# Rearranging the first chunk of a fused linear-attention and MLP kernel: PSUM banks, load order, attention slots and constants

## The chip, the cores and the metric

The kernel runs on one core of a Trainium2 chip. The metric is the device time in microseconds of one execution. The kernel before takes 301.79 us (median of 3 runs, 301.38 to 301.83). A profile is one execution taken by the hardware profiler; its span is some 1.8 us shorter than the time (299.9 us for the kernel before, in an execution of 301.66 us). Times within a profile count from the start of its span.

## The reference, cut to what matters

```
phi(x) = where(x > 0, x, exp(x) - 1) + 1          # q, k, v: 8 batches, 8 heads, 576 tokens, 64 wide
kv  = sum over tokens of phi(k) v                  z = sum over tokens of phi(k)
num = phi(q) kv                                    den = phi(q) z + 1e-6
x = num / den, heads side by side                  # 4608 tokens x 512
h = x @ w_in ; g = h - tanh(h) ; out = g @ w_out   # 512 -> 2048 -> 512
```

Inputs and output are float32; the kernel multiplies in bfloat16. A load from GpSimd's queue casts on its way (18.35 MB counted on that queue for 36.7 MB of inputs).

## The kernel before

TensorE is busy nearly all the time, so the kernel runs the two layers of the MLP without a break, in 9 chunks of 512 tokens, and slips the attention of later batches between their matmuls. A chunk has a first layer (16 blocks of 4 matmuls, each block followed by a tanh on ScalarE and a subtraction on VectorE) and a second layer (16 steps of 4 matmuls). Lists `s1[block]` and `s2[step]` hold what is emitted after a block or a step. In the traces each engine runs its instructions in the order in which the kernel emits them (in the changed kernel VectorE subtracts for the tenth block at 27.48 us and does what stands in that block's slot at 28.09 us), so a slot in these lists is also a place in VectorE's and ScalarE's queues.

The divisor of the attention has to be spread from one row per head to 64 rows per head. Batches 0 and 1, which are urgent, do that by matmuls with a selector ("spread"); later batches send 1/den out to memory and read it back broadcast (`ds`, then `rdb`).

The opening, with the PSUM banks it uses (first index of the free part of `ps_all`):

```
def b0_z(i):        # sum of phi(k):  ps_all[:, 2*i + hg, 0:32]
def b0_kv(i):       # phi(k) v:       ps_all[:, 4 + 2*i + hg, 0:128]
def b0_num(i, ns):  # numerators:     banks 2 and 3; the last 64 tokens in bank 1
    ...
def b0_spread(pairs, n0):          # 1/den of two head pairs into banks 4 to 7
    for n, p in enumerate(pairs):
        for t in range(4):
            nc.tensor.matmul(ps_all[:, 4 + t, 128 * (n0 + n):128 * (n0 + n) + 128], sel..., rden...)
def b0_scale(p, ns, n):            # x of one head pair = numerator * spread
    nc.vector.tensor_mul(xT[:, p, 0:512]..., ns[:, p, 0:8]..., ps_all[:, 4:8, 128 * n:128 * n + 128]...)
...
b0_spread((0, 2), 0); b0_scale(0, ns0, 0); b0_scale(2, ns0, 1)
b0_num(1, ns0)
b0_spread((1, 3), 2); b0_scale(1, ns0, 2); b0_scale(3, ns0, 3)
```

The loads, in the order of GpSimd's queue:

```
load_q(0); make_identity(nc, ident); load_k(0); load_v(0)
for g in range(4): load_wi(g)
load_k(1); load_wo(0); load_wo(1); load_q(1); load_wo(2); load_v(1); load_wo(3)
```

The slots of chunk 0, in which batch 1 is worked off, and of chunk 1 (`n1` is batch 2 there):

```
s2[3].append(lambda: a_qphi(1, 0)); s2[5].append(lambda: a_qphi(1, 1))
s2[6].append(lambda: a_qT_pe(1, 0, side)); s2[7].append(lambda: a_qT_pe(1, 1, side))
s2[10].append(lambda: a_kv(1, side))
s2[12].append(lambda: (a_den(1, side), num1(), a_split(1)))
s2[14].append(lambda: spread1(0))
s2[15].append(lambda: (spread1(1), a_qphi(2, 0), a_qphi(2, 1), a_qT_dma(2)))
...
s1[8 if c == 1 else 5].append(lambda: a_kv(n1, attn))
s1[11 if c == 1 else 8].append(lambda: (a_den(n1, attn), a_spread(n1)))
for p in range(NP + 1):
    s2[(11 if c == 1 else 9) + p].append(lambda p=p: a_num(n1, p))
```

## Time and profile before

| | before |
|---|---|
| time | 301.79 us |
| span of the profile | 299.9 us |
| TensorE busy | 288.8 us, 96% |
| VectorE, ScalarE, GpSimd busy | 181.9, 150.2, 48.7 us |
| first matmul of the first layer | 19.24 us |
| chunk 0, second layer begins | 33.07 us |
| chunk 1, first layer begins | 52.57 us |
| chunk 1, second layer begins | 70.05 us |
| chunk 2 begins | 86.25 us |

TensorE is the bound. What can be won is the time in which it stands still, and that lies in the first 86 us alone. So the way to read this profile is not by shares of the span, but stage by stage: where a stage is longer than its matmuls, and what ended the wait there. The prediction below shows those lines.

### The profile page before, as it was taken

To read this page: it belongs to the slowest core of one execution; us is meant where nothing else is said; L and a number is where in the kernel's file an instruction comes from. 1 tells how busy PE (TensorE), PEld (TensorE's weight loads), DVE (VectorE), ACT (ScalarE), POOL (GpSimd) and SP (SyncE) were. 2 spreads that over 40 slices of the span, in tenths; PEclk is the share of its full clock that TensorE was granted. 3 is DMA by queue.
4 is the path that set the end of the run, shared out by engine and by line. 5 is a ranking of instruction groups with operands and counts; after the bars stand their busy time and mean duration, and the time that the engine had idled before them with its cause. 6 is when DMAs were issued, how large, how long until landed. Compare 5 with 4: busy or idle time off the path is not lost.

```text
span 299.9 us, 4765 instructions
## 1 busy us (share of the span) xinstructions
PE 288.8 (96%) x1804; PEld 137.4 (46%) x1804; DVE 181.9 (61%) x320; ACT 150.2 (50%) x234; POOL 48.7 (16%) x87
## 2 busy tenths in 40 slices
PE   8889999989989999999999999999999999999994
PEld 3444453444435444544454445444544444444443
DVE  4769936997467854785478557865682467007600
ACT  4637836856434653565256625662562166126411
POOL 8823150060015000600060006000000000000000
PEclk9999999999999999999999999999999999999999
DMA  6999999669889776968696777977108310131033
GB/s 96 183 206 213 205 206 221 161 99 163 193 185 158 135 177 142 153 114 191 142 148 118 193 150 102 173 182 160 37 4 192 73 35 0 37 77 28 0 72 70
DMA packets 39126, 38.95 MB, mean 130 GB/s; under 512 B 16896, under 2 KB 33856, under 8 KB 38336
## 3 DMA queue, kind: packets, MB, share of 16 engines
q0 software_dynamic: 17600, 18.35, 38.2%
q1 hardware_dynamic: 21504, 20.31, 29.8%
q8 instruction: 14, 0.23, 0.3%
q14 instruction: 8, 0.07, 0.1%
HBM read 43.91 MB, written 9.55 MB: 178 GB/s over the span
## 4 chain that ended last, share of the span: by engine, by line
PE 83%; DMA 6%; DVE 6%; POOL 2%; issue 1%; ACT 1%; SPq 0%; DVEq 0%; POOLq 0%; ACTq 0%
PE ps_all L356 38%; PE ps_all L371 35%; PE ps_all L179 3%; DMA rdb<-ds 3%; DMA kraw<-in_k_dram 2%; PE ps_all L307 2%; DMA ds<-rden 2%; PE ps_all L566 1%; DVE gT L362 1%; PE ps_all L263 1%; POOL qraw L88 1%; DVE kp L138 1%; DVE xT L349 1%; DVE rden L275 1%; POOL kraw L88 1%
## 5 line engine op out<-in xcount | busy, mean ns | idle before, releaser
L356 PE MATMUL ps_all<-xT,w_in_sb 128*128 128x512 bf16 x576 | 127.9, 379 | 0.0
L371 PE MATMUL ps_all<-w_out_sb,gT 128*128 128x512 bf16 x560 | 127.7, 379 | 0.0
L362 DVE TENSOR_TENSOR gT<-ps_all,th 128x512 bf16<-128x512 f32 x144 | 96.4, 686 | 47.8 <-ACT th L361 47.2
L361 ACT ACTIVATE th<-ps_all 128x512 f32<-128x512 f32 x144 | 85.2, 597 | 52.0 <-PE ps_all L356 45.2
L356 PEld LDWEIGHTS <-w_in_sb 128*128 128x128 bf16 x576 | 55.1, 98 | 66.4 <-issue 0.9
L371 PEld LDWEIGHTS <-gT 128*128 128x128 bf16 x560 | 54.2, 98 | 65.6 <-issue 1.7
L377 ACT COPY osb<-ps_all 128x512 f32<-128x512 f32 (+1 forms) x37 | 21.2, 577 | 83.6 <-PE ps_all L371 66.7
L318 DVE TENSOR_TENSOR xT<-ps_all,rdb 128x512 bf16<-128x512 f32 x24 | 16.3, 688 | 15.8 <-PE ps_all L307 12.2
L107 POOL DMA_DIRECT2D v<-in_v_dram x32 | 19.3, 647 | 7.6 <-DMA w_out_sb<-in_moe_w_out_dram 2.3
L136 ACT ACTIVATE e<-qraw 128x1152 bf16<-128x1152 bf16 x16 | 18.4, 1160 | 2.2 <-DMA qraw<-in_q_dram 2.2
L367 POOL COPY g<-gT 1x1 bf16<-1x1 bf16 x5 | 0.9, 176 | 109.4 <-DVE gT L362 109.4
L138 DVE TENSOR_TENSOR kp<-e,r 128x1152 bf16<-128x1152 bf16 x15 | 11.4, 757 | 12.0 <-ACT e L136 11.1
L136 ACT ACTIVATE e<-kraw 128x1152 bf16<-128x1152 bf16 x15 | 17.4, 1161 | 0.0
L138 DVE TENSOR_TENSOR qp<-e,r 128x1152 bf16<-128x1152 bf16 x16 | 12.1, 758 | 7.8 <-ACT e L136 6.9
L179 PE MATMUL ps_all<-v,kp 64*128 64x192 bf16 x252 | 11.8, 243 | 1.2 <-DVE kp L138 1.2
L179 PEld LDWEIGHTS <-kp 64*128 64x128 bf16 x252 | 10.0, 94 | 4.5 <-issue 2.5
L307 PE MATMUL ps_all<-qT,kz 128*128 128x512 bf16 x28 | 10.1, 379 | 1.2 <-DVE xT L318 1.2
L420 PE MATMUL ps_all<-zero 128*128 128x512 bf16 x32 | 9.3, 452 | 1.2 <-DVE zero L384 1.2
L92 POOL DMA_DIRECT2D qraw<-in_q_dram x14 | 8.7, 634 | 8.8 <-DVE r L137 4.9
L92 POOL DMA_DIRECT2D kraw<-in_k_dram x14 | 8.7, 626 | 8.2 <-ACT th L361 4.9
L188 DVE TENSOR_TENSOR kz<-ps_all,mask 128x320 bf16<-128x320 f32 x14 | 6.2, 484 | 5.2 <-PE ps_all L179 5.2
L137 DVE TENSOR_SCALAR r<-qraw 128x1152 bf16<-128x1152 bf16 x16 | 7.3, 454 | 2.2 <-DMA qraw<-in_q_dram 2.2
(78 smaller groups left out, 98.6 us busy)
## 6 DMA issues: line engine op xcount, KB each, us to landing
out_dram<-osb SPq DMA_DIRECT2D x70, 128.0 KB
rdb<-ds SPq DMA_DIRECT2D x12, 576.0 KB
v<-in_v_dram POOLq DMA_DIRECT2D x32, 144.0 KB, 8.0
kraw<-in_k_dram POOLq DMA_DIRECT2D x14, 288.0 KB, 5.0
qraw<-in_q_dram POOLq DMA_DIRECT2D x14, 288.0 KB, 7.2
w_in_sb<-in_moe_w_in_dram POOLq DMA_DIRECT2D x4, 512.0 KB, 10.9
w_out_sb<-in_moe_w_out_dram POOLq DMA_DIRECT2D x4, 512.0 KB, 16.6
qraw<-in_q_dram POOLq DMA_DIRECT2D x4, 144.0 KB, 3.9
```

Of the source, the lines that this page charges most:

```text
L92: nc.gpsimd.dma_start(out=t[64 * hg:64 * hg + 64].rearrange("p i h j d -> p (i h) (j d)"), in_=src[b, 4 * hg:4 * hg + 4].rearrange("h (p j ...
L107: nc.gpsimd.dma_start(out=v_b[b % 2][64 * hg:64 * hg + 64, i, 0:2].rearrange("p h j d -> p h (j d)"), in_=v[b, h0:h0 + 2].rearrange("h (p ...
L136: return (lambda: nc.scalar.activation(e, x, AF.Exp), lambda: nc.vector.tensor_scalar(r, x, 0.0, 1.0, ALU.max, ALU.add), lambda: nc.vector ...
L138: lambda: nc.vector.tensor_tensor(y, e, r, ALU.min))
L179: nc.tensor.matmul(ps[hg], kp[r, i, j].rearrange("p h d -> p (h d)"), vt[r, i, :, j, :], start=(j == 0), stop=(j == J - 1))
L307: nc.tensor.matmul(ps, kz[:, p // 2, p % 2, 0:128], qT[:, p % 2, 0:8, p // 2, :], start=True, stop=True)
L318: nc.vector.tensor_mul(xT[:, p, S * b:S * b + 512].rearrange("p (j t c) -> p j t c", j=8, t=4), ps.rearrange("p j (t c) -> p j t c", t=4), ...
L356: nc.tensor.matmul(h, w_in_sb[:, p, fi * 128:(fi + 1) * 128], xT[:, p, c * 512:(c + 1) * 512], start=(n == 0), stop=(n == NP - 1))
L361: nc.scalar.activation(th, h, AF.Tanh)
L362: nc.vector.tensor_sub(gT[:, fi, :], h, th)
L371: nc.tensor.matmul(o, gT[:, fi, i * 128:(i + 1) * 128], w_out_sb[:, fi, :], start=(fi == 0), stop=(fi == NF - 1))
L377: nc.scalar.copy(osb[:, f0:f1], o[:, f0:f1])
```

## The change

The intent: let the opening wait for less (kv and numerators in banks 0 to 3, the spread in banks 4 to 7, two first-layer matmuls between the two spreads), bring the attention of batch 1 half a layer forward so that its last steps don't stand at the end of chunk 0, load q of batches 1 and 2 ahead of w_out so that this is possible, and take two memsets off VectorE.

```diff
     def b0_z(i):
-                nc.tensor.matmul(ps_all[:, 2 * i + hg, 0:32], ...
+                nc.tensor.matmul(ps_all[:, 4 + 2 * i + hg, 0:32], ...
     def b0_kv(i):
-                nc.tensor.matmul(ps_all[:, 4 + 2 * i + hg, 0:128], ...
+                nc.tensor.matmul(ps_all[:, 2 * i + hg, 0:128], ...
     def b0_num(i, ns):
-        for hg in range(2):
-            nc.tensor.matmul(ps_all[:, 1, 64 * hg:64 * hg + 64], ...      # the last 64 tokens
...
-            nc.tensor.matmul(ps_all[:, 2 + hg, :]...
+            nc.tensor.matmul(ps_all[:, b0 + hg, :]...                     # b0 = 2 * i
-        nc.scalar.copy(ns[:, i::2, 8, :], ...
-    def b0_scale_rest(ns):
+    def b0_scale_rest(banks):
+        ps = num_mm(0, NP, banks)                                         # the last 64 tokens, later
     load_q(0)
+    load_k(0)
     make_identity(nc, ident)
-    load_k(0)
...
     load_k(1)
+    load_q(1)
+    for i in (1, 0):
+        nc.gpsimd.memset(v_b[i][:, :, 2], 1.0)
     load_wo(0)
     load_wo(1)
-    load_q(1)
+    load_v(1)
     load_wo(2)
-    load_v(1)
-    load_wo(3)
...
-            s1[6].append(lambda: b0_scale_rest(ns0))
-            s1[12].append(lambda: a_kphi(1, 0))
...
+            s1[9].append(lambda: b0_scale_rest(first))
+            s1[10].append(lambda: a_kphi(1, 0))
+            s1[12].append(lambda: a_kphi(1, 1))
+            s1[14].append(lambda: a_qphi(1, 0))
+            s2[1].append(lambda: (a_qphi(1, 1), load_q(2), load_wo(3), load_k(2), load_v(2)))
+            s2[2].append(lambda: a_qT_pe(1, 0, side))
+            s2[3].append(lambda: a_qT_pe(1, 1, side))
+            s2[4].append(prepare)
+            s2[5].append(lambda: a_kv(1, side))
+            s2[7].append(lambda: a_den(1, side))
+            s2[8].append(lambda: (num1(), a_split(1)))
+            s2[10].append(lambda: (spread1(0), a_qphi(2, 0)))
+            s2[12].append(lambda: (spread1(1), a_qphi(2, 1), a_qT_dma(2)))
+            s2[15].append(lambda: a_kphi(2, 0))
...
-            s1[8 if c == 1 else 5].append(lambda: a_kv(n1, attn))
-            s1[11 if c == 1 else 8].append(lambda: (a_den(n1, attn), a_spread(n1)))
+            s1[6 if c == 1 else 5].append(lambda: a_kv(n1, attn))
+            s1[9 if c == 1 else 8].append(lambda: (a_den(n1, attn), a_spread(n1)))
...
-            s1[4].append(lambda: a_kphi(2, 0))
-            s1[5].append(lambda: a_kphi(2, 1))
+            s1[1].append(lambda: a_kphi(2, 1))
...
-            first = Banks([4, 5, 6, 7, 0, 1, 2, 3])
+            first = Banks([4, 5, 6, 7, 0, 1, 2, 3, 2, 4, 5, 6, 7])
+                if n == 1:
+                    open2()                    # second spread, after two first-layer matmuls
```

The two memsets and the selector work on VectorE are gone from the opening; the selector work is now `prepare`. Chunk 1 no longer interleaves its first four blocks.

More of the change, by code (lines that the diff above doesn't have):

```diff
@@ L195, in b0_z @@
                 r = slice(64 * hg, 64 * hg + 64)
-                nc.tensor.matmul(ps_all[:, 2 * i + hg, 0:32], kp_t[0][r, i, j].rearrange("p h d -> p (h d)"),
+                nc.tensor.matmul(ps_all[:, 4 + 2 * i + hg, 0:32], kp_t[0][r, i, j].rearrange("p h d -> p (h d)"),
                                  one[r, 0:32], start=(j == 0), stop=(j == J - 1))
     def b0_zc(i):
-        nc.vector.tensor_mul(kz_t[0][:, :, i, 128:160], ps_all[:, 2 * i:2 * i + 2, 0:32], mask[:, :, i, 128:160])
+        nc.vector.tensor_mul(kz_t[0][:, :, i, 128:160], ps_all[:, 4 + 2 * i:6 + 2 * i, 0:32], mask[:, :, i, 128:160])
     def b0_kv(i):
@@ L206, in b0_kv @@
                 r = slice(64 * hg, 64 * hg + 64)
-                nc.tensor.matmul(ps_all[:, 4 + 2 * i + hg, 0:128], kp_t[0][r, i, j].rearrange("p h d -> p (h d)"),
+                nc.tensor.matmul(ps_all[:, 2 * i + hg, 0:128], kp_t[0][r, i, j].rearrange("p h d -> p (h d)"),
                                  v_b[0][r, i, 0:2, j, :], start=(j == 0), stop=(j == J - 1))
     def b0_kz(i):
-        nc.vector.tensor_mul(kz_t[0][:, :, i, 0:128], ps_all[:, 4 + 2 * i:6 + 2 * i, 0:128], mask[:, :, i, 0:128])
+        nc.vector.tensor_mul(kz_t[0][:, :, i, 0:128], ps_all[:, 2 * i:2 * i + 2, 0:128], mask[:, :, i, 0:128])
     def b0_num(i, ns):
-        kz, qT = kz_t[0], qT_t[0]
+        kz, qT, b0 = kz_t[0], qT_t[0], 2 * i
         for hg in range(2):
-            nc.tensor.matmul(ps_all[:, 1, 64 * hg:64 * hg + 64], kz[:, hg, i, 0:128], qT[:, i, 8, hg, :],
-                             start=True, stop=True)
-        for hg in range(2):
-            nc.tensor.matmul(ps_all[:, 2 + hg, :].rearrange("p (j t) -> p j t", j=8), kz[:, hg, i, 0:128],
+            nc.tensor.matmul(ps_all[:, b0 + hg, :].rearrange("p (j t) -> p j t", j=8), kz[:, hg, i, 0:128],
                              qT[:, i, 0:8, hg, :], start=True, stop=True)
-        nc.scalar.copy(ns[:, i::2, 8, :], ps_all[:, 1, 0:128].rearrange("p (a t) -> p a t", a=2))
-        nc.scalar.copy(ns[:, i::2, 0:8, :].rearrange("p a j t -> p a (j t)"), ps_all[:, 2:4, :])
+        nc.scalar.copy(ns[:, i::2, 0:8, :].rearrange("p a j t -> p a (j t)"), ps_all[:, b0:b0 + 2, :])
     def b0_spread(pairs, n0):
@@ L239, in b0_rest @@
     def b0_rest():
-        nc.vector.reciprocal(rden_t[0][:, 128:144], ps_all[:, 0, 128:144])
         ds = dram.tile([H, 4, 16], F32, name="ds0")
@@ L250, in b0_rest @@
         rdb_t[0] = rdb
-    def b0_scale_rest(ns):
+    def b0_scale_rest(banks):
+        ps = num_mm(0, NP, banks)
         nc.vector.tensor_mul(
             xT[:, :, 512:576].rearrange("p a (t c) -> p a t c", t=4),
-            ns[:, :, 8, :].rearrange("p a (t c) -> p a t c", t=4), rdb_t[0])
+            ps[:, 0:NP, :].rearrange("p a (t c) -> p a t c", t=4), rdb_t[0])
     def a_den(b, banks):
@@ L273, in a_den @@
         rden = rpool.tile([128, J * 16], F32, name="rden")
-        n = J * 16 if b > 0 else 128
-        nc.vector.reciprocal(rden[:, 0:n], den[:, 0:n])
+        nc.vector.reciprocal(rden, den)
         rden_t[b] = rden
@@ L419, in spin @@
         for _ in range(n):
-            nc.tensor.matmul(ps_all[:, 2, :], zero[:, 0:128], zero, start=True, stop=True)
-    for t in range(4):
-        nc.scalar.copy(s8[32 * t:32 * t + 32, 0].rearrange("q h p -> q (h p)"),
-                       ident[32 * t:32 * t + 32, 32 * t:32 * t + 8])
+            nc.tensor.matmul(ps_all[:, 0, :], zero[:, 0:128], zero, start=True, stop=True)
     side = Banks([4, 5, 6, 7])
@@ L439 @@
         f()
+    for t in range(4):
+        nc.scalar.copy(s8[32 * t:32 * t + 32, 0].rearrange("q h p -> q (h p)"),
+                       ident[32 * t:32 * t + 32, 32 * t:32 * t + 8])
     nc.scalar.copy(sel, s8[:, 0].rearrange("q h p -> q p h").unsqueeze(3).to_broadcast([128, NP, 2, 64]))
@@ L449 @@
     b0_zc(1)
-    a_den(0, Banks([0]))
+    a_den(0, Banks([4]))
     ns0 = new_ns(0)
+    b0_rest()
     b0_num(0, ns0)
@@ L454 @@
     b0_kz(1)
-    b0_rest()
     b0_spread((0, 2), 0)
@@ L459, with open2, prepare @@
     b0_num(1, ns0)
-    b0_spread((1, 3), 2)
-    b0_scale(1, ns0, 2)
-    b0_scale(3, ns0, 3)
-    nc.vector.memset(v_b[1][:, :, 2], 1.0)
-    nc.vector.memset(v_b[0][:, :, 2], 1.0)
-    for t in range(4):
-        nc.vector.tensor_copy(s8[32 * t:32 * t + 32, 1:3].rearrange("q n h p -> q (n h p)"),
-                              ident[32 * t:32 * t + 32, 32 * t + 8:32 * t + 24])
-    s24 = rpool.tile([128, 2 * NP], F32, name="s24")
-    f8 = s8.rearrange("q n h p -> q n (h p)")
-    nc.vector.tensor_add(s24, f8[:, 1], f8[:, 2])
-    nc.vector.tensor_reduce(part[:, 0:1], s24, mybir.AxisListType.X, ALU.add, negate=True)
-    nc.vector.tensor_reduce(part[:, 1:2], f8[:, 2], mybir.AxisListType.X, ALU.add, negate=True)
-    nc.vector.tensor_add(s24, s24, f8[:, 0])
-    nc.vector.tensor_copy(
-        sel3, s24.rearrange("q (h p) -> q p h", h=2).unsqueeze(3).to_broadcast([128, NP, 2, 64]))
-    load_q(2)
-    load_k(2)
-    load_v(2)
+    def open2():
+        b0_spread((1, 3), 2)
+        b0_scale(1, ns0, 2)
+        b0_scale(3, ns0, 3)
+    def prepare():
+        for t in range(4):
+            nc.vector.tensor_copy(s8[32 * t:32 * t + 32, 1:3].rearrange("q n h p -> q (n h p)"),
+                                  ident[32 * t:32 * t + 32, 32 * t + 8:32 * t + 24])
+        s24 = rpool.tile([128, 2 * NP], F32, name="s24")
+        f8 = s8.rearrange("q n h p -> q n (h p)")
+        nc.vector.tensor_add(s24, f8[:, 1], f8[:, 2])
+        nc.vector.tensor_reduce(part[:, 0:1], s24, mybir.AxisListType.X, ALU.add, negate=True)
+        nc.vector.tensor_reduce(part[:, 1:2], f8[:, 2], mybir.AxisListType.X, ALU.add, negate=True)
+        nc.vector.tensor_add(s24, s24, f8[:, 0])
+        nc.vector.tensor_copy(
+            sel3, s24.rearrange("q (h p) -> q p h", h=2).unsqueeze(3).to_broadcast([128, NP, 2, 64]))
     for c in range(NC):
@@ L498, in num1 @@
                     a_num_copy(1, sub["ns"], p, side)
-            s1[6].append(lambda: b0_scale_rest(ns0))
-            s1[12].append(lambda: a_kphi(1, 0))
-            s1[14].append(lambda: a_kphi(1, 1))
-            s2[3].append(lambda: a_qphi(1, 0))
-            s2[5].append(lambda: a_qphi(1, 1))
-            s2[6].append(lambda: a_qT_pe(1, 0, side))
-            s2[7].append(lambda: a_qT_pe(1, 1, side))
-            s2[10].append(lambda: a_kv(1, side))
-            s2[12].append(lambda: (a_den(1, side), num1(), a_split(1)))
-            s2[14].append(lambda: spread1(0))
-            s2[15].append(lambda: (spread1(1), a_qphi(2, 0), a_qphi(2, 1), a_qT_dma(2)))
+            s1[9].append(lambda: b0_scale_rest(first))
[12 more added lines that the diff above has]
+            s2[15].append(lambda: a_kphi(2, 0))
         elif n1 < B:
-            s1[8 if c == 1 else 5].append(lambda: a_kv(n1, attn))
-            s1[11 if c == 1 else 8].append(lambda: (a_den(n1, attn), a_spread(n1)))
+            s1[6 if c == 1 else 5].append(lambda: a_kv(n1, attn))
+            s1[9 if c == 1 else 8].append(lambda: (a_den(n1, attn), a_spread(n1)))
             for p in range(NP + 1):
@@ L527 @@
         if c == 0:
-            first = Banks([4, 5, 6, 7, 0, 1, 2, 3])
-            hs = [ps_all[:, fi, :] for fi in range(4)]
-            order = [(0, 0), (0, 1), (2, 0), (2, 1), (0, 2), (0, 3), (2, 2), (2, 3)]
-            order += [(p, fi) for p in (1, 3) for fi in range(4)]
-        elif c == 1:
-            hs = [dense() for fi in range(4)]
-            order = [(p, fi) for p in range(NP) for fi in range(4)]
-        if c < 2:
-            seen = [0] * 4
-            for p, fi in order:
-                l1mm(c, fi, hs[fi], p, seen[fi])
-                seen[fi] += 1
+            first = Banks([4, 5, 6, 7, 0, 1, 2, 3, 2, 4, 5, 6, 7])
+            hs = [ps_all[:, n, :] for n in range(4)]
+            order = [((0, 0), (0, 1)), ((2, 0), (2, 1), (0, 2), (0, 3), (2, 2), (2, 3)),
+                     [(p, fi) for p in (1, 3) for fi in range(4)]]
+            seen = [0] * 4
+            for n, part_ in enumerate(order):
+                if n == 1:
+                    open2()
+                for p, fi in part_:
+                    l1mm(c, fi, hs[fi], p, seen[fi])
+                    seen[fi] += 1
             for fi in range(4):
                 l1act(fi, hs[fi], gT)
-            for fi in range(4):
-                for f in s1[fi]:
-                    f()
-        for fi in range(4 if c < 2 else 0, NF):
+        for fi in range(4 if c == 0 else 0, NF):
             h = first() if c == 0 else dense()
```

## The prediction

> **What bounds the kernel now.** I read the page first (engines, then the clock row, which is 9 in all 40 slices), then who TensorE waited for, then the busy time by stage, then the timeline of the stages with a gap, and last the DMA landings.
>
> ```profile
> PE 288.8 (96%) x1804; PEld 137.4 (46%) x1804; DVE 181.9 (61%) x320; ACT 150.2 (50%) x234; POOL 48.7 (16%) x87
> ```
>
> TensorE is the bound. From 86.25 us on, the chain is TensorE without a gap, and the change leaves that code alone. So it can only win in the first 86 us. The waits of TensorE:
>
> ```profile
> PE ps_all L307 <- DVE xT L318: 1.2, 1, 1.2
> PE ps_all L179 <- DVE kp L138: 1.2, 2, 0.9
> ...
> PE ps_all L230 <- DVE xT L234: 0.9, 1, 0.9
> ...
> PE ps_all L344 <- DVE xT L349: 0.6, 1, 0.6
> ```
>
> Columns: who waited for whom, us in total, times, longest. These four are the whole prize: 3.9 us, plus slivers. By stage (the first layer of chunk 0, its second layer, first and second layer of chunk 1):
>
> ```profile
> 19.24:33.07 13.83, 13.83 (x69) 6.29 (x66) 13.10 (x27) 8.56 (x15) 3.73 (x6) 1.00 1.24 210
> 33.07:52.57 19.50, 18.77 (x159) 9.44 (x158) 12.05 (x24) 10.87 (x19) 5.59 (x9) 1.00 1.21 212
> 52.57:69.50 16.93, 15.68 (x121) 7.54 (x115) 16.00 (x28) 11.79 (x19) 5.01 (x9) 1.00 0.73 137
> 69.50:86.40 16.90, 15.65 (x77) 7.04 (x76) 8.99 (x15) 7.13 (x10) 0.00 (x0) 1.00 0.93 197
> ```
>
> Columns: stretch, its length, busy PE, PEld, DVE, ACT, POOL, clock, DMA share, GB/s. In the first two stretches the DMA moves 210 GB/s and its share stands at 1.2: it is saturated there, while TensorE has hardly a gap. That is the second bound to watch. In the third DVE is full (16.00 of 16.93). The opening of the first stage:
>
> ```profile
> 15.82 1.31 PE L230 MATMUL ps_all<-rden,sel 32*128 32x128 f32 x16
> ...
> 16.41 0.52 PEld L230 LDWEIGHTS ps_all<-rden,sel 32*128 32x128 f32 x12 [0.30 <-DVE kz L211]
> ...
> 17.24 1.29 DVE L234 TENSOR_TENSOR xT<-ns,ps_all 128x512 bf16<-128x512 f32 x2 [0.72 <-PE ps_all L230]
> ...
> 18.58 0.73 PE L230 MATMUL ps_all<-rden,sel 32*128 32x128 f32 x16 [0.86 <-DVE xT L234]
> ```
>
> The first spread of 1/den takes 1.31 us instead of the 0.73 us of the second: 12 of its 16 matmuls wait for the kz multiply to leave banks 6 and 7. The second spread then waits 0.86 us for the scaling of two heads.
>
> **What the Trainium skill says.** "PSUM — Partial Sum Buffer", PSUM bank collisions raise a hardware error: two engines may not touch the same bank and quadrant at once, even in disjoint columns, and a scheduler adds a dependency for it. The trace agrees: the second spread writes columns 256 to 511 of banks 4 to 7, the scaling reads 0 to 255, and yet it waits. "TensorE: Matmul & The Clock Gate", Wait — 56ns, not 53.3ns?: 215.7 ns from start to start of warm 512-column matmuls; here 64 take 13.83 us, 216 ns each. "DMA: Bandwidth & Descriptors", Where 436 GB/s comes from: a ceiling of 435 GB/s. The loads read float32 and write bfloat16 (36.7 MB of inputs, 18.35 MB counted on the GpSimd queue), so 210 GB/s is about 420 GB/s read: agrees, the loads can't go faster, only in another order. "SBUF — State Buffer", Who interferes with whom: VectorE with at most one SBUF input, outside its two-port modes, does not contend with GpSimd. The kz multiply and the scaling have one PSUM input and float32, so memsets on GpSimd should not slow them; no line of before shows it.
>
> **Part 1, the PSUM banks of batch 0.** kv and num move to banks 0 to 3, z and den to 4 to 7, so the first spread need not wait for the second kz multiply. The reciprocal starts at 14.71 and grows from 128 to 144 columns (0.96 to 1.05 us), ending at 15.76. The spread runs from 15.82 to 16.55 in place of 17.13: 0.58 us sooner. Scaling of heads 0 and 2 (1.29 us) then runs from 16.62 to 17.91. In the built kernel two first-layer matmuls stand between the scaling and the second spread; they fill part of the old wait. The spread runs 17.96 to 18.70, and the other 62 matmuls follow. Against 19.24 that is a start at 18.70 less 2 x 0.216 = 18.27: 0.97 us gained. The two small numerator matmuls per half and their 0.27 us ACT copies vanish, four matmuls (0.12 us) come back within the first layer as the late rest of batch 0. Moving k's load ahead of the identity (0.27 and 0.29 us on GpSimd) might gain 0 to 0.4 us; k's landings trail its issues by 4.7 to 5.4 us against 3.2 for the first q, so they queue behind data and I count nothing. First layer over at 18.27 + 13.83 + 0.12 = 32.2 instead of 33.07.
>
> **Part 2, the loads.** The first w_out quarter is what the second layer needs first. Before:
>
> ```profile
> L117 POOL DMA_DIRECT2D w_out_sb<-in_moe_w_out_dram x1: 759/759/759, 14.3 to 14.3; - x1
> ...
> DMA to landing us min/median/max: 17.1/17.1/17.1
> ```
>
> It lands at 14.3 + 17.1 = 31.4, in front of 33.07. Now both halves of q of batch 1 go ahead of it; by the landings of before (33.7 for the second w_out quarter, 35.0 and 36.4 for these halves) that is 2.7 us on the same saturated queue. With k of batch 1 landed at 28.5: q at 31.3, w_out 0 at 33.9, w_out 1 at 36.4, v of batch 1 at 39.2, w_out 2 at 41.8; then q of batch 2 at 44.7, w_out 3 at 47.2, k at 50.2, v at 53. So TensorE, ready at 32.2, waits 1.7 us for w_out: a new wait that eats the gain of part 1 and 0.7 us more. The other pieces are in time by my stage times below (the nearest, v of batch 1, by about 0.9 us).
>
> **Part 3, attention of batch 1 sooner.** The second layer of chunk 0 then starts at 33.9. Its work: 64 x 0.216 = 13.8, transposes 1.0, kv 1.6, den 0.4, num 1.0, spread 0.7: 18.4 us. Before it took 19.5, the rest being the waits around the two spreads at 50.4 and 52.3. Now den comes after step 7 of 16 instead of 12 and the last spread after step 12 instead of 15, so VectorE's reciprocal and split (2.75 us) and the 1.42 us of scaling are covered. End at 52.3 against 52.57. VectorE is relieved by two memsets of 1.02 us and has the 1.6 us of selector work later, where it idles. Rest of the kphi of batch 2 comes before the third tanh of chunk 1, so the first layer there has no wait for kp: 64 x 0.2165 + 1.6 + 0.4 = 15.85 us instead of 70.05 - 52.57 = 17.48. End at 68.15. Lastly the numerators:
>
> ```profile
> 75.26 7.86 DMA rdb<-ds
> ...
> 83.24 0.70 DVE xT L318
> ...
> 83.98 0.38 PE ps_all L307
> ```
>
> The chain of waits shows 1/den of batch 2 going out to memory and back: reciprocal done at 68.95, broadcast landed at 83.1, 14.2 us. The den step moves two steps forward and the stage is earlier: reciprocal done near 65.2, landed by 79.4 or sooner, as the loads of batch 3 start some 5 us earlier too and collide with it less. The third numerator wants it at about 80; so no wait, and the second layer of chunk 1 takes 13.8 + 1.0 = 14.8 us instead of 16.2. End at 82.95 instead of 86.25.
>
> **Sum.** Chunk 0 by its end 0.3 us, first layer of chunk 1 1.6, second 1.4: 3.3 us. From there each step is as before. 301.8 - 3.3 = 298.5 us.
>
> **The rivals.** (a) w_out is no bound: the early loads run at only 150 to 190 GB/s before 14 us, so k ahead of the identity might shift the whole queue by some tenths, and the order of service might favour the weights. Then up to 1.7 us more is won: 296.8 us. Against it: before, every landing follows its predecessor on the saturated queue by size. (b) The DMA wait grows or hits again, at w_out 3 (a margin of 1.3 us) or v of batch 1, because stores or the 1/den round trip of batch 0 take bandwidth: 1 to 1.5 us lost, 299.5 to 300. (c) VectorE becomes the bound of the crossing into chunk 1: it must do two scalings, two phis of q, two of k and the tanh subtractions there. By my count kp is ready 1.0 us ahead of its matmuls. If not, the 1.6 us of the third stage are won only in part: 299.5. (d) The broadcast of batch 2 lands late still; then 1.2 us stay: 299.7. (e) GpSimd's memsets (1.6 us each, an estimate from 0.10 us for 1 column and 0.27 for 128) delay the w_out issue; the queue then still holds w_in, k and q, so nothing comes of it.
>
> **Range and chances.** The mechanisms are separate tenths to 1.7 us each; all failing leaves the time as it is, all succeeding with no w_out wait makes 296.8. I put 298.4 us, range 296.6 to 300.2. Two per cent is 6 us, more than all the waits of before hold: 4% faster, 95% same, 1% slower.
>
> **What would show it.** The spread without a split at about 15.8 and the first layer's main run from about 18.7; a TensorE idle of 1 to 2 us in front of the first second-layer matmul, released by a w_out load; none in front of the later spreads, the kv of batch 2, or the third numerator; last of all, the steady stretch of the same length as before, shifted by about 3.3 us. The prediction is wrong if the w_out wait is missing (then faster) or if a new VectorE wait stands at the crossing into chunk 1.

## The result

The changed kernel takes 298.84 us (median of 4 runs, 298.22 to 299.20) against 301.81 us (4 runs). The ratio is 0.9898, 95% interval 0.9872 to 0.9924: 1% faster, inside the 2% that counts as the same. Ratios here are the mean time of one kernel's fast runs over that of the other's of the same rounds, so not quite the ratio of the medians that I quote. The predicted 298.4 us was 0.4 us too low.

The page's first line for the changed kernel, and who TensorE waited for (columns: who, for whom, us in total, times, longest):

```profile
PE 286.4 (96%) x1774; PEld 137.3 (46%) x1804; DVE 180.6 (61%) x317; ACT 149.5 (50%) x232; POOL 51.4 (17%) x89
```

```profile
PE ps_all L366 <- DMA w_out_sb<-in_moe_w_out_dram: 1.3, 1, 1.3
...
PE ps_all L351 <- DVE xT L249: 0.8, 1, 0.8
```

All four waits of before are gone from the list, save 0.2 us at the second spread and 0.3 us of the two matmuls ahead of it for their x. Two new ones came: 1.3 us for the first w_out quarter, which was forecast, and 0.8 us of first-layer matmuls for the scaling of the rest of batch 0 (line 249), which was not. (The count of matmuls is lower than before because some records are missing from the trace; the weight loads are 1804 in both.)

The four stages, by busy time (columns as before: stretch, length, PE, PEld, DVE, ACT, POOL, clock, DMA share, GB/s):

```profile
18.44:34.37 15.93, 13.79 (x70) 6.18 (x68) 12.79 (x22) 11.30 (x19) 3.89 (x6) 1.00 1.23 209
34.37:53.01 18.64, 18.27 (x155) 9.34 (x158) 13.42 (x33) 9.05 (x15) 5.58 (x9) 1.00 1.18 198
53.01:68.99 15.98, 15.87 (x115) 7.78 (x116) 13.80 (x24) 11.10 (x18) 5.01 (x9) 1.00 0.99 180
68.99:83.79 14.80, 14.69 (x72) 6.78 (x73) 8.63 (x14) 6.58 (x8) 0.00 (x0) 1.00 0.87 194
```

The first stretch is now the one with the hole: 15.93 us with 13.79 busy. The other three are nearly full. VectorE in the third fell from 16.55 to 13.80 us of work, as part of it moved forward into the second. (The 16.55 us are for 52.57 to 70.05 us, where that stage ended; the prediction's row, with 16.00, stops at 69.50.)

The opening in the timeline of TensorE (columns: start, duration, what, how many, and in brackets the idle time before it with what ended it):

```profile
15.59 0.73 PE L226 MATMUL ps_all<-rden,sel 32*128 32x128 f32 x16
...
17.18 0.38 PE L351 MATMUL ps_all<-xT,w_in_sb 128*128 128x512 bf16 x1 [0.33 <-DVE xT L230]
17.78 0.73 PE L226 MATMUL ps_all<-rden,sel 32*128 32x128 f32 x16 [0.22 <-DVE xT L230]
18.44 8.38 PE L351 MATMUL ps_all<-xT,w_in_sb 128*128 128x512 bf16 x37
...
28.56 4.48 PE L351 MATMUL ps_all<-xT,w_in_sb 128*128 128x512 bf16 x20 [0.76 <-DVE xT L249]
34.37 2.75 PE L366 MATMUL ps_all<-w_out_sb,gT 128*128 128x512 bf16 x12 [1.33 <-DMA w_out_sb<-in_moe_w_out_dram]
```

The first spread is one piece of 0.73 us, and the first layer's main run starts at 18.44. Ahead of 28.56 it stands still for 0.76 us, and at its end for 1.33 us. The chain of waits says the same of the second stop (columns: start, duration, what):

```profile
17.17 17.15 DMA w_out_sb<-in_moe_w_out_dram
```

The chain of before ran through the opening's matmuls and multiplies; this one runs through the loads' issue, with the two memsets of GpSimd (1.95 us) in it, and, for 17 us, through the load of w_out. What the memsets are worth there is answered by the run with them back on VectorE. What the first layer does before 34.32 us does not set the end any more, in this execution.

| stage begins at, us | before | predicted | after |
|---|---|---|---|
| first layer, chunk 0 (less the 2 matmuls done early) | 19.24 | 18.27 | 18.01 |
| second layer, chunk 0 | 33.07 | 33.9 | 34.37 |
| first layer, chunk 1 | 52.57 | 52.3 | 53.01 |
| second layer, chunk 1 | 70.05 | 68.15 | 68.99 |
| chunk 2 | 86.25 | 82.95 | 83.79 |
| end of the span | 299.9 | | 297.4 |

From chunk 2 to the end both take 213.6 us. So the gain in the profile, 2.46 us, is made in chunk 1 alone; by the end of chunk 0 the changed kernel is even 0.44 us behind.

### The profile page after: what moved, and what is told of

It reads as the page before. It is cut to its first block, busy times and chain, and to the rows that moved or that the text cites. A ratio compares the mean times of both kernels' runs of the same rounds, so it can differ in the third digit from the quotient of the medians.

```text
span 297.4 us, 4732 instructions
## 1 busy us (share of the span) xinstructions
PE 286.4 (96%) x1774; PEld 137.3 (46%) x1804; DVE 180.6 (61%) x317; ACT 149.5 (50%) x232; POOL 51.4 (17%) x89
## 3 DMA queue, kind: packets, MB, share of 16 engines
q0 software_dynamic: 17600, 18.35, 38.8%
## 4 chain that ended last, share of the span: by engine, by line
PE 86%; DMA 6%; POOL 5%; issue 1%; ACT 0%; POOLq 0%
PE ps_all L366 40%; PE ps_all L351 37%; DMA w_out_sb<-in_moe_w_out_dram 6%; PE ps_all L179 4%; PE ps_all L302 2%; PE ps_all L559 1%; POOL w_in_sb L113 1%; PE ps_all L259 1%; POOL qraw L88 1%; POOL v L107 1%; POOL kraw L88 1%; POOL v L391 1%; POOL kraw L92 0%; POOL qraw L92 0%; PE ps_all L166 0%
## 5 line engine op out<-in xcount | busy, mean ns | idle before, releaser
L366 PE MATMUL ps_all<-w_out_sb,gT 128*128 128x512 bf16 x547 | 125.8, 379 | 2.2 <-DMA w_out_sb<-in_moe_w_out_dram 1.3
L313 DVE TENSOR_TENSOR xT<-ps_all,rdb 128x512 bf16<-128x512 f32 x24 | 16.5, 690 | 14.2 <-PE ps_all L302 14.2
L138 DVE TENSOR_TENSOR kp<-e,r 128x1152 bf16<-128x1152 bf16 x15 | 11.4, 758 | 13.3 <-ACT e L136 12.6
```

The lines of the kernel that those rows point to most:

```text
L138: lambda: nc.vector.tensor_tensor(y, e, r, ALU.min))
L313: nc.vector.tensor_mul(xT[:, p, S * b:S * b + 512].rearrange("p (j t c) -> p j t c", j=8, t=4), ps.rearrange("p j (t c) -> p j t c", t=4), ...
L366: nc.tensor.matmul(o, gT[:, fi, i * 128:(i + 1) * 128], w_out_sb[:, fi, :], start=(fi == 0), stop=(fi == NF - 1))
```

## The experiments

The theory: (1) the late attention slots were the whole gain; (2) the load order put a wait for w_out in place of what the opening won, so the banks bring nothing. Rivals: the loads or the banks carry the gain; or the w_out wait costs nothing. Each kernel but the last is the changed one with one or a few edits. All gave correct results. The calls ran on three different chips. The changed kernel itself ran again in the third call alone (the control), so where a run of the first two is compared with it, 298.84 us is from another call; differences of some tenths of a us are to be read with that in mind.

### w_out ahead of q of batch 1

```diff
     load_k(1)
+    load_wo(0)
     load_q(1)
     ...memsets...
-    load_wo(0)
     load_wo(1)
```

> The first w_out quarter is loaded ahead of q of batch 1, all else as changed. Theory (order on a saturated queue): it lands 2.6 us sooner, near 31.8, so the 1.33 us wait in front of the second layer of chunk 0 vanishes and that layer starts at 33.0; but q of batch 1 lands near 34.4 in place of 31.8, so the transposes of step 2 wait some 0.8 us and those of step 3 another 0.3 to 0.6 us for q's phi, and of the 1.3 us only 0 to 0.4 us reach the end: ratio to the changed kernel 0.998 to 1.000, about 298.5 us. Rival (only w_out binds): the full 1.3 us, 297.5 us. Rival (the wait is not a matter of the order): it stays at 1.3 us.

298.88 us (298.54 to 299.18), ratio 0.9905 (0.9889 to 0.9921): no change, as expected. The first w_out quarter lands at 14.5 + 16.9 = 31.4 us instead of 34.3, and TensorE's timeline has no wait at the second layer, but two for q's phi:

```profile
36.48 0.68 PE L166 MATMUL ps_all<-ident,qp 128*128 128x128 bf16 x9 [0.20 <-DVE qp L138]
...
38.30 0.68 PE L166 MATMUL ps_all<-ident,qp 128*128 128x128 bf16 x9 [0.29 <-DVE qp L138]
```

In this execution the first layer itself started at 19.09, 0.65 us later than in the profile of the changed kernel; that fits the two waits, smaller than expected, and the second layer's start at 33.52. More on this under the control run.

### The same, with the attention a step later

```diff
-            s2[2], s2[3]: transposes; s2[4] prepare; s2[5] kv; s2[7] den; s2[8] numerators; s2[10], s2[12] spreads
+            s2[3], s2[4]: transposes; s2[5] prepare; s2[6] kv; s2[8] den; s2[9] numerators; s2[11], s2[13] spreads
```

> As the run before, and attention of batch 1 one step later (transposes at steps 3 and 4, kv 6, den 8, numerators 9, spreads 11 and 13). Theory: q's phi is then ready when TensorE asks, the second layer starts at 33.0 and needs 18.6 us, end at 51.7 in place of 53.0: 1.2 to 1.4 us faster than the changed kernel, about 297.5 us. Rival (something else, w_out 1, v of batch 1 or the last scaling, binds next): a wait of 0.3 to 1 us there, 298 to 298.5 us.

298.25 us (297.84 to 298.32), ratio 0.9881 (0.9863 to 0.9899). Its four runs all lie below the four of the kernel above, on the same chip, so 0.6 us are won; half of what I expected. The stage's own length is what I expected, 18.65 us, without a wait in it:

```profile
33.40:52.05 18.65, 18.65 (x160) 9.36 (x158) 13.72 (x33) 10.21 (x16) 5.59 (x9) 1.00 1.21 205
```

Of what is missing, 0.4 us is at its start: 33.40 and not 33.0, as the opening of this execution was 0.5 us later. With the wait for w_out gone, nothing stands between the first layer and the second in this trace that could hide a late opening.

### The rest of batch 0 sooner, in another bank

```diff
-            s1[9].append(lambda: b0_scale_rest(first))
+            s1[8].append(lambda: b0_scale_rest(first))
-            first = Banks([4, 5, 6, 7, 0, 1, 2, 3, 2, 4, 5, 6, 7])
+            first = Banks([4, 5, 6, 7, 0, 1, 2, 3, 1, 4, 5, 6, 7])
```

In the changed kernel the rest is written to bank 2 after the tenth block, and the twelfth block (the expectation says the eleventh) needs bank 2 again; VectorE reads it only after it has done the subtraction of the tenth block. Here the rest goes to bank 1 one block sooner.

> The rest of batch 0 one step sooner and in the bank of a step before, so that the eleventh first-layer block does not need its bank at once. Theory: the 0.76 us wait for that bank vanishes or falls to 0.2 us, the first layer ends near 32.4 instead of 33.04, and the wait for w_out grows by the same to about 1.9 us: no change of the time (within 0.2 us). Rival (waits add up): 0.6 to 0.8 us faster.

298.97 us (298.80 to 299.09), ratio 0.9908 (0.9893 to 0.9923): no change. The bank wait is gone from the list, the 28 matmuls from 26.26 us on are one piece, and the wait for w_out stands:

```profile
33.96 2.75 PE L366 MATMUL ps_all<-w_out_sb,gT 128*128 128x512 bf16 x12 [1.44 <-DMA w_out_sb<-in_moe_w_out_dram]
```

The first layer began 0.35 us later than in the profile of the changed kernel and yet ended sooner, and TensorE waited 1.44 us for the load. So the 0.76 us wait cost nothing that shows: with a load behind it that lands when it lands, whatever TensorE does before, the two waits don't add up.

### Banks and opening of before

The functions of the opening, their banks, the order of the opening and the rest of batch 0 as in the kernel before; loads, slots and memsets as changed.

```diff
-    a_den(0, Banks([4])); ns0 = new_ns(0); b0_rest(); b0_num(0, ns0); b0_kv(1); b0_kz(1)
+    a_den(0, Banks([0])); ns0 = new_ns(0); b0_num(0, ns0); b0_kv(1); b0_kz(1); b0_rest()
-                if n == 1:
+                if n == 0:
                     open2()
```

> The PSUM banks and the opening of batch 0 as in the kernel before (numerators of the rest, two small copies, spread waiting for kz, both spreads ahead of the first layer), the other parts as changed. Theory: the first layer starts near 18.9 instead of 18.0 (k stays 0.3 us sooner), has no wait for the rest's bank, ends near 32.8, and waits for w_out until 34.3: the time of the changed kernel within 0.2 us, so the new banks bring nothing while w_out binds. Rival (the opening counts in full): 0.9 us slower, near 299.7 us.

299.38 us (298.79 to 300.77), ratio 0.9925 (0.9905 to 0.9944). That is 0.5 us over the changed kernel by the medians, between the two expectations, and the intervals overlap. The trace (of the slowest of the six runs) shows how a late first layer can count in spite of w_out. Not all of its lateness is the old opening's: it starts at 19.77, 1.76 us after the changed kernel's 18.01, but the z matmuls, ahead of the part that was changed, already start 0.85 us later (13.23 instead of 12.38), which belongs to the run (see the control). The w_out quarter lands at 18.0 + 15.7 = 33.7 and the first layer ends at 33.72, so there is no wait for it; but then:

```profile
38.06 0.68 PE L166 MATMUL ps_all<-ident,qp 128*128 128x128 bf16 x9 [1.58 <-DVE qp L138]
```

VectorE does the phi of q between the subtractions of the first layer, so a late first layer makes phi late, and it stood still 0.96 us for the broadcast of the rest's 1/den as well. My theory that the opening is worth nothing here is too strong: w_out hides it on TensorE's path only as long as VectorE's path is shorter. What the opening itself is worth, this run does not settle.

### The late slots again

`s2`: transposes 6 and 7, `prepare` 8, kv 10, den, numerators and split 12, spreads 14 and 15; in chunk 1 kphi of batch 2 at 4 and 5, kv 8, den 11, first four blocks interleaved.

> Banks, loads and constants as changed, but the attention of batch 1 at the late steps of before, kphi of batch 2 and den of batch 2 too (first four blocks of chunk 1 interleaved as before). Theory (part 3 is the whole gain): the waits around the two spreads (1.1 us), for kp of batch 2 (about 1.5) and for 1/den of batch 2 (1.2) come back; with w_out still late it ends 0.5 to 1.5 us slower than before, 302.3 to 303.3 us. Rival (loads or banks carry the gain): 299 to 300.5 us.

302.52 us (301.89 to 303.81), ratio 1.0039 (1.0018 to 1.0060): slower than before, as the theory said. TensorE's waits:

```profile
PE ps_all L179 <- DVE kp L138: 1.3, 2, 0.9
...
PE ps_all L302 <- DVE xT L313: 0.9, 1, 0.9
...
PE ps_all L339 <- DVE xT L344: 0.6, 1, 0.6
```

The three waits of before are back (kp of batch 2, the third numerator, the second spread of batch 1), and one of 0.6 us for w_out stays. Banks, loads and memsets without the slots (the phi of batch 1 stays early here) gain nothing and lose 0.9 us by the medians. So the change is not faster without the slots. The reverse, the slots with the loads of before, was not run: there q of batch 1 lands at 35.0 and 36.4 us, and the changed kernel's phi takes it up at 33.28 and 34.81.

### Only kv and den of batch 2 late

```diff
-            s1[6 if c == 1 else 5].append(lambda: a_kv(n1, attn))
-            s1[9 if c == 1 else 8].append(lambda: (a_den(n1, attn), a_spread(n1)))
+            s1[8 if c == 1 else 5].append(lambda: a_kv(n1, attn))
+            s1[11 if c == 1 else 8].append(lambda: (a_den(n1, attn), a_spread(n1)))
```

> Only kv and den of batch 2 at steps 8 and 11 of chunk 1 again. Theory (the sooner den removes the wait of the third numerator): the reciprocal ends near 67.9 instead of 66.2, and with the 14.2 us from there to the landing of before the broadcast lands at 82.1, 0.7 to 1.5 us late for the third numerator: 0.7 to 1.5 us slower than the changed kernel. Rival (the loads of batch 3 that start 5 us sooner and are out of the way shorten the round trip to under 12.5 us): no wait, the same time within 0.2 us.

299.42 us (298.89 to 300.34), ratio 0.9930 (0.9915 to 0.9944): 0.6 us over the changed kernel. The trace, though, has no wait at the numerators:

```profile
80.81 2.13 DVE L313 TENSOR_TENSOR xT<-ps_all,rdb 128x512 bf16<-128x512 f32 x3 [1.95 <-DMA rdb<-ds]
```

```profile
81.83 0.38 PE L302 MATMUL ps_all<-qT,kz 128*128 128x512 bf16 x1
```

VectorE waited 1.95 us for the broadcast, until 80.81, and the scaling that frees the bank ended at 81.50, 0.33 us before the third numerator. From the end of the reciprocal (67.16 + 1.05 = 68.21) to there it took 12.6 us; before it was 14.2. So both theories hold in part: the round trip is 1.6 us shorter though den is late, and that just suffices here; the sooner den adds the margin. That the loads of batch 3 make it shorter, which are issued sooner (from 58.07 us here and 57.75 in the changed kernel, 62.29 before), was not tested alone, but four traces fit it. The first leg, from the first write of 1/den to memory to the first read back, took 5.75 us before and 5.65 us with the late slots, where the last of these loads was issued 1.85 us ahead of it; 5.24 us in the changed kernel, 3.6 us ahead; 4.05 us here, 5.3 us ahead. In this execution the first layer of chunk 0 began at 19.65 us, the latest of all with the new opening, and that fits its time better than the moved slots do. Whether a run with a sooner opening has a wait at the numerators I did not see; what the 0.6 us are stays open.

### The identity between q and k

```diff
     load_q(0)
-    load_k(0)
     make_identity(nc, ident)
+    load_k(0)
```

> The identity between the loads of q and k of batch 0 again. Theory: kp is 0.3 us later (first z matmul at 12.7 instead of 12.38), but the affine select takes 0.29 instead of 0.83 us, as no VectorE multiply with two SBUF inputs runs beside it, v and w_in follow 0.3 us sooner and w_out lands 0.2 to 0.4 us sooner; as w_out binds, the end is 0.2 to 0.4 us sooner. Rival (the opening counts): 0.3 us later.

299.12 us (298.71 to 300.47), ratio 0.9930 (0.9909 to 0.9951): not faster, and the interval overlaps with that of the changed kernel. Four of its runs are at 298.7 to 299.3 and two at 300.3 and 300.5. In its trace the affine select of the identity takes 0.29 us, w_out lands a little sooner (the wait ends at 34.12 instead of 34.37; but in the control, with k first, at 33.62), and the z matmuls start at 12.55 instead of 12.38. Inconclusive alone; it was repeated below, where it could count.

### The memsets back on VectorE

```diff
-    for i in (1, 0):
-        nc.gpsimd.memset(v_b[i][:, :, 2], 1.0)
...
         b0_scale(3, ns0, 3)
+        for i in (1, 0):
+            nc.vector.memset(v_b[i][:, :, 2], 1.0)
```

> The two memsets of the ones of v on VectorE again, at the place of before. Theory: 2.04 us of VectorE at 19.9, of which 1.7 us lie in its idle time before the first tanh; the rest is caught up, the first layer's length and the end are unchanged within 0.2 us. Rival (VectorE or GpSimd's issue of w_out binds there): up to 2 us slower, or, if the memsets hold up the loads, up to 1 us faster.

298.61 us (298.38 to 299.23), ratio 0.9905 (0.9892 to 0.9919): no change, as expected. Moving the constants to GpSimd neither gains nor loses that one can see: VectorE has the time there. The rival that the memsets hold up w_out is answered by its trace (GpSimd's timeline):

```profile
16.89 0.75 POOL L117 DMA_DIRECT2D w_out_sb<-in_moe_w_out_dram  x1 [1.57 <-DMA w_in_sb<-in_moe_w_in_dram]
```

Without the memsets GpSimd waits for the w_in loads to land before it issues this one, and issues it only 0.28 us sooner than in the changed kernel's profile (17.17) and 0.54 us sooner than in the control's (17.43). It landed at 33.4 us, and TensorE did not wait for it. On GpSimd the two took 2.11 us, on VectorE 2.04 (1.02 each).

### Both: w_out first with the later slots, and the rest sooner

The idea is to take out at once what the runs above showed to bind: the edits of "w_out ahead of q" and "the rest sooner", with slots 3 and 5 for the transposes, 5 for `prepare`, and 6, 8, 9, 11, 13 for the others.

> First w_out quarter ahead of q of batch 1, attention of batch 1 a step later (second transposes two steps), and the rest of batch 0 sooner in another bank. Theory: with w_out out of the way the 0.76 us of the bank wait are now on the path, the second layer starts 0.7 us sooner than with the first two changes alone: 297.3 to 297.8 us, ratio to before about 0.986. Rival (q of batch 1, v of batch 1 or VectorE binds within the second layer): as with the two changes alone, 298.2 us.

297.63 us (297.50 to 298.21), ratio 0.9868 (0.9840 to 0.9896). The fastest, in the range expected: all five of its runs lie below all five of the control. Its profile is of its slowest run and shows the next limits:

```profile
36.40 0.68 PE L166 MATMUL ps_all<-ident,qp 128*128 128x128 bf16 x9 [0.55 <-DVE qp L138]
...
48.22 1.89 PE L366 MATMUL ps_all<-w_out_sb,gT 128*128 128x512 bf16 x7 [0.33 <-DMA w_out_sb<-in_moe_w_out_dram]
```

The second layer starts at 32.22, 2.15 us sooner than in the changed kernel's profile, and gives 0.88 us of it back to q's phi and to the last w_out quarter.

### Both, with the old opening

The kernel above with the opening of before, as under "Banks and opening of before".

> The run before with the banks and opening of before. Theory: with no wait for w_out behind it, the opening counts nearly in full: 0.7 to 1.0 us slower than the run before. Rival (the transposes' wait for q's phi takes w_out's place and hides the opening): within 0.3 us of the run before.

298.42 us (297.47 to 299.48), ratio 0.9891 (0.9858 to 0.9924). By the medians 0.8 us slower than the kernel above, as the theory has it, but its runs scatter over 2 us and the intervals overlap. Its trace speaks for the rival: the second layer starts 1.05 us later (33.27 instead of 32.22; 0.31 us of it is there in the z matmuls already, 12.91 instead of 12.60), and chunk 0 still ends at 51.92 against 52.02, as the waits of the kernel above are not there. So the worth of the new banks lies between nothing and 0.8 us, and these runs don't settle it.

### Both, with the identity between q and k

> The run before the last with the identity between the loads of q and k of batch 0. In the eight traces with k first, the second half of q is ready between 7.84 and 9.18 us (mean 8.34) and the first z matmul starts at 12.84 in the mean; in the two with the identity between, 7.67 and 7.86, and 12.71 and 12.55. Theory (k sooner only takes bandwidth from q): the same time within 0.3 us or up to 0.4 us faster, with the second half of q at 7.6 to 7.9 again. Rival (k sooner is a gain of 0.3 us): slower by that.

297.80 us (297.19 to 298.96), ratio 0.9872 (0.9845 to 0.9900): the same as with k first. The z matmuls start at 13.14 in its trace. Over all traces they start at 12.81 us in the mean of the eleven with k first, and at 12.80 in the mean of the three with the identity between, the kernel before among them (12.71, 12.55, 13.14). Moving k's load ahead of the identity brings nothing that shows. What k gains, q may lose: its second half is ready at 8.34 us in the mean of the eleven and at 7.83 in the mean of the three.

### The control

The changed kernel, not edited.

> The changed kernel as it is, on the same chip as these runs: ratio 0.990 within 0.002, with the second half of q of batch 0 ready anywhere between 7.8 and 9.2 us. If that readiness is a property of the kernel and not of the run, it is 7.86 again.

298.62 us (298.40 to 299.20), ratio 0.9898 (0.9870 to 0.9926): the first result repeated. But its trace is not the same. The second half of q of batch 0 is ready at 8.30 us and not 7.86, the first layer starts at 18.77 and not 18.44, and the wait for w_out is

```profile
33.62 2.75 PE L366 MATMUL ps_all<-w_out_sb,gT 128*128 128x512 bf16 x12 [0.25 <-DMA w_out_sb<-in_moe_w_out_dram]
```

0.25 us and not 1.33: the load landed 0.75 us sooner and the first layer was 0.33 us later. So when the first loads land is a property of the run, not of the kernel. The 1.33 us are one execution's. In the eight traces of kernels with this load order (k before or after the identity), the first w_out quarter lands between 33.4 and 34.4 us, and the wait is between none (three of them) and 1.44 us; the changed kernel's profile has the latest landing of all. That may be why (it was not tested) the kernels without the wait win only 0.6 us (a step later) and 1.0 us (with the rest sooner as well) by the medians.

## Why the prediction was right

**What bounds, and where the prize lies.** Right. The stretch after chunk 2 has the same 213.6 us in both.

**Part 1, the banks.** The mechanism was right and the size nearly: the first spread runs in one piece, and the first layer starts 1.23 us sooner instead of 0.97. The difference is chance: the z matmuls start 0.33 us sooner than before (12.38), in the control they do not (12.71), and there the first layer starts at 18.34 by the same count, 0.90 us sooner. The step that failed is "four matmuls (0.12 us) come back within the first layer": the rest of batch 0 cost 0.12 us of matmuls and a 0.76 us wait for its bank. I had counted the matmuls and not asked when VectorE would free the bank they write to. The run with the rest in another bank shows that the miss cost nothing behind the w_out wait; that the time came out as said in spite of it was luck. Once the w_out wait is out of the way, the first layer is shorter without the miss by 0.87 us (13.56 us in place of 14.43 in the traces of "Both" and "The same, with the attention a step later"), though the times of those two, 297.63 and 298.25 us, come from different calls and their intervals overlap.

**Part 2, the loads.** Right in kind: TensorE waited 1.33 us for the first w_out quarter, where I said 1.7 us. It landed at 34.3 instead of 33.9, as the stream ran later as a whole in this execution: the second half of k of batch 1 landed at 13.4 + 15.8 = 29.2 and not at 28.5, v having been issued at 7.19 instead of 6.62 us (0.54 us of that is the slower affine select, see below). The other loads were in time, as said. The size is only good for one execution, as the control shows, and I had given it as if it were fixed. Two slips in the sums: 31.4 + 2.7 is 34.1 and not 33.9, and by my own times the wait eats the gain of part 1 at the first layer's end (33.07 - 32.2) and 0.8 us more, not 0.7. That the loads "can't go faster" I had read from the closeness of 420 GB/s to the 435 of "DMA: Bandwidth & Descriptors"; but the page gives that ceiling for the SBUF ports, over which these casting loads bring half of that, so the closeness does not show what limits them. What the traces show is 210 and 212 GB/s over the first two stages before, 209 and 198 after.

**Part 3, attention sooner.** Right, and shown by the run with the late slots (1.0039). The second layer of chunk 0 took 18.64 us (18.4 said), the first of chunk 1 15.98 (15.85), the second 14.80 (14.8). (The second layer's terms sum to 18.5, not 18.4; and the last two rows of my table by stage were cut at 69.50 and 86.40 us, where the stages end at 70.05 and 86.25.) My reason for the last was only half right. I had the reciprocal done near 65.2 us; it was done at 66.16, 2.8 us sooner than before. The first leg of the round trip was 0.5 us shorter as well. Here the sooner den is the larger part, but the run with den late shows that it was not needed: there the shorter round trip alone took the wait away.

**Sum.** 3.3 us said; 2.46 us by the profiles, 2.97 us by the medians. The terms: w_out later by 0.47, chunk 0's second layer longer by 0.24, chunk 1's first by 0.13, together 0.84 us in the profiles.

**Rivals.** (a), that w_out is no bound, fell for the profiled run, but the control (0.25 us) comes near it, and with the memsets on VectorE the wait, whose absence was to be a sign of being wrong, is missing from the profile, with a time that is no different (298.61 us). (b) to (d) did not occur. (e) was right: memsets on GpSimd change nothing; my estimate of 1.6 us each was too high, they took about 1.05.

**The pages of the Trainium skill.** The rule on banks in "PSUM — Partial Sum Buffer", PSUM bank collisions raise a hardware error, fits the old wait at the second spread (0.86 us, disjoint columns of banks 4 to 7). The new one at bank 2 needs no such rule: there the block writes the very columns that the scaling reads. "SBUF — State Buffer", Who interferes with whom, also says that a VectorE instruction with two SBUF inputs contends with a GpSimd instruction that reads SBUF, and that the one that starts first holds the port to its end. The traces agree: the affine select starts at 6.41 to 6.43 us in all eleven traces with k first. Where the multiply of phi (two SBUF inputs, 0.76 us) had started before it, at 6.32 and 6.38, the select took 0.83 and 0.88 us; where the multiply started at 6.48 or later, 0.29. The other side shows too: the six multiplies that start at 6.48 to 6.54, while the select runs, all end at 7.30 to 7.32 and take up to 0.83 us, as if each had been held to about 6.55 (estimated: 7.31 less 0.76); with the identity ahead of k, so that no select runs then, one that starts at 6.52 takes 0.76. Here is the changed kernel's timeline:

```profile
6.32 0.76 DVE L138 TENSOR_TENSOR qp<-e,r 128x1152 bf16<-128x1152 bf16 x1 [0.51 <-ACT e L136]
```

```profile
6.41 0.83 POOL masks.py:199 TENSOR_SCALAR_AFFINE_SELECT ident<-ident 128x128 bf16<-128x128 bf16 x1
```

## What to carry to other kernels

When a wait is taken away ahead of a point where a load lands at a time that does not depend on it, ask first what of it reaches past that point; here, in the profiled execution, the opening's gain stopped at w_out, and the gain of the change came from slots behind it. A load order is a budget: with the two halves of q ahead of it the first w_out quarter landed at 33.4 to 34.4 us, without them at 30.5 to 31.4. The best version here loads that quarter first, gives the displaced q one and two steps more, and moves the rest of batch 0 to another bank (297.63 us). And take more than one profile before believing the size of a wait near the start of a kernel: it varied between 0.25 and 1.33 us in the same kernel.

## What the Trainium skill lacked or had wrong

- "DMA: Bandwidth & Descriptors", Where 436 GB/s comes from, says without a condition that for loads from HBM the HBM side, about 358 GB/s, binds. With one core active the DMA moved 209 to 210 GB/s in the first stage, nearly all of it casting loads written as bfloat16, so 400 to 420 GB/s read as float32 (estimated from the 18.35 MB counted for 36.7 MB of inputs), above that figure. The page is not wrong as a whole: where it gives its measurements it says that 358 GB/s is a core's share when both cores of a pair stream. I found no page with a figure for loads that cast.
- "GPSIMD Engine Reference", Engine selection, calls one-input work roughly line-rate, and has no figure for a memset. Two of 128 x 1152 bfloat16 took 2.11 us on GpSimd against 2.04 on VectorE, which agrees; an extrapolation from small memsets (1.6 us each) did not.
- None of the pages that I read says how much the landing of the first loads varies from run to run. In the eleven traces with k loaded right after q, the second half of q was ready between 7.84 and 9.18 us.
